# Attention and two MLPs on one core: loads that write 32 partitions each, issued half by SyncE and half by GpSimd

## The chip, the cores and the metric

The kernel runs on one core of one Trainium2 chip. The metric is device microseconds of one execution, from launch to end. Of the kernel before, three runs took 1405.77, 1406.9 and 1407.61 us; the median is 1406.9 us.

## What is computed

```python
def _attn_ref(u, v, z):                      # u, v: (2, 3008, 256), z: (2, 3008, 64)
    scores = (1.0 / S) * np.matmul(z, z.transpose(0, 2, 1))
    attn = np.maximum(scores, 0.0) ** 2
    return u * np.matmul(attn, v)

def _moe_ref(x, w_in, w_out, s, b):          # 6016 tokens, 256 -> 2048 -> 256
    r = np.maximum(x @ w_in, 0.0)
    return (s * (r * r) + b) @ w_out

def _moe2_ref(x, w_in, w_out):
    h = x @ w_in
    return (h * (1.0 / (1.0 + np.exp(-1.702 * h)))) @ w_out
```

The output is `_moe2_ref(_moe_ref(attention))`. Products on TensorE are made of two-part splits of float32 (a high part `hi` in float32r and the rest, `lo`), three matmuls for one product.

## The kernel before, in words

**Attention.** Each of the two batches has its 3008 tokens cut into six column chunks of 512 (the last has 448). For a query chunk `c` and a key chunk `kc`, four steps (`t`, 128 keys each) go through scores (L545, two matmuls into `ps_s`), relu and square on ScalarE (L549, L552), the split (`hi` L556 on ScalarE, `lo` L560 on VectorE) and six matmuls with `v` into an accumulator (L484, L485, L489). The scores are symmetric, so a block `(kc, c)` off the diagonal is computed once (`Fresh`), and its **mirror image** serves the other side: VectorE transposes the squared scores in 32x32 blocks into a tile `T` (L585), `park` stores it in HBM as `H` (L600, 128 partitions, 1 MB, from GpSimd's queue), and `fetch` (L604) loads it back as `R` in another arrangement: four DMAs of 256 KB, each to 32 of the 128 partitions (L613, from SyncE's queue). A `Turned` step then takes `hi` and `lo` out of `R` (L635, L639). `T` and `R` share five buffers of 1 MB (the pool `wide`); there are 15 such images in each batch.

**Other loads to 32 partitions.** `load_z` (L347) brings a chunk of `z` in four DMAs of 64 KB (runs of 128 bytes) to 32 partitions each, `load_v` (L420) a chunk of `v` in four DMAs of 128 KB (runs of 1 KB), `load_u` (L900) a chunk of `u` in four DMAs of 128 KB (runs of 256 bytes). All are SyncE's, but for the first chunks of `z` and `v`, shared with ScalarE's queue, and the other chunks of `v` in the first batch, which are GpSimd's and wait for `go`: a small copy on GpSimd (L400) after the first transposed `z`.

**Weights and MLPs.** The weights come as float64; VectorE and ScalarE decode them to float32 (`decode`, L656) and make sums and splits of them (`prepare`, L728) in the gaps of the attention and of the first MLP; GpSimd's queue stores these forms (L785 to L806), and SyncE's queue loads them for the MLPs (L815, L828, L842, L845). The two MLPs run from about 460 us to the end, in pairs of token chunks, with a seven-product scheme (L1088 up, L1256 and L1281 down).

**What sets the order.** Every piece of work is put on a list by `put` (L309) with its engine, its cost and the keys that it reads and writes; loads go through `moves` (L321), which gives them a transfer time `pipe`, scaled by a factor `slow`. A planner, `ordered` (L31), simulates the engines with these costs, free buffers and eight DMAs in flight in each of two sets (`lanes`, one for GpSimd's queue) and writes one order of all pieces. Each engine then runs its instructions in that order. In the built program the DMAs of a queue take eight semaphores in turn, so that a ninth waits for the landing of the first.

Of the kernel before, what the change touches and what calls it, by code (L numbers as in the profile page):

```python
# [20 lines left out]
class Op:  # L21


    def __init__(self, engine, cost, late, f, reads, writes, new, adds, free, due, pipe, soon, count):
        self.engine, self.cost, self.late, self.f = engine, cost, late, f
        self.reads, self.writes, self.new, self.adds = list(reads), list(writes), list(new), list(adds)
        self.free, self.due, self.pipe, self.soon, self.count = free, due, pipe, soon, count
        self.keys = list(dict.fromkeys(self.reads + self.writes + self.adds))


def ordered(ops, counts, clocks, reach, ahead, bulk, spread):  # L31
# [40 lines left out]
            before[users[new][0]].update(users[old])  # L72
    for i in range(n):
        before[i].discard(i)
        for j in before[i]:
            after[j].append(i)

    def lag(j, i):
        a = ops[j]
        if a.engine == ops[i].engine:  # L80
            return a.cost if a.engine == "PE" else a.cost + 0.1
        return a.cost + a.late
# [75 lines left out]
    while len(result) < n:  # L158
        best = None
        for e, now in clocks.items():  # L160
            among = [i for i in line[:reach] if not waiting[i]] if e == "PE" else pending[e]
            s0, pick = None, None
            soon = []
            for i in among:
                if best is not None and ready[i] >= best[0]:
                    continue
                t = start_of(i, now)
                if t is None:
                    continue
                t = max(t, now)  # L170
                rank = i if e == "PE" else latest[i]
                soon.append((rank, t, i))
                if s0 is None or t < s0 - 1e-9 or (t <= s0 + 1e-9 and rank < s0_rank):
                    s0, pick, s0_rank = t, i, rank
            if pick is not None and e in YIELD:
                limit = s0 + YIELD[e] * ops[pick].cost
                for rank, t, i in soon:
                    if t < limit and rank < s0_rank - WORTH and rank < t + URGENT:
                        s0, pick, s0_rank, limit = t, i, rank, 0.0 if t > s0 else limit
                        break  # L180
            if pick is not None and (best is None or s0 < best[0]):
                best = s0, pick, e
        if best is None:
            raise RuntimeError(f"no order: {len(result)} of {n}, {[(k, len(x)) for k, x in slots.items()]}, {left}")
        s0, i, e = best
        op = ops[i]
        end, late = s0 + op.cost, op.late
        if op.pipe:
            time, land, lane = s0, 0.0, lanes[e == "POOL"]
            for _ in range(op.count):  # L190
                time = max(time, lane.pop(0))
                pipe = max(pipe, time + 0.4) + op.pipe / op.count
                time += op.cost / op.count
                lane.append(max(time + 1.9, pipe + 1.7))
                land = max(land, lane[-1])
            end = time
            late = land - end
        clocks[e] = end
        (line if e == "PE" else pending[e]).remove(i)
        result.append(i)  # L200
        starts.append(s0)
        for key, kind in op.new:
            slots[kind].pop(0)
            needs[kind].remove((latest[i], i))
            if op.free and kind in left:
                left[kind] -= 1
                taken[key] = kind
        for key in op.keys:
            if key in uses:
                u = uses[key]  # L210
                u[1] -= 1
                u[2] = max(u[2], end + late)
                if u[1] == 0:
                    slots[u[0]].append(u[2])
                    if key in taken:
                        left[taken[key]] += 1
        for j in after[i]:
            waiting[j] -= 1
            t = end + late if op.pipe else s0 + lag(i, j)
            ready[j] = max(ready[j], t)  # L220
            if ops[j].free or op.engine != ops[j].engine:
                calm[j] = max(calm[j], t + (SLACK[0] if ops[j].free and op.pipe else SLACK[1] if op.pipe else SLACK[2]))
            if not waiting[j] and ops[j].engine != "PE":
                pending[ops[j].engine].append(j)
# [4 lines left out]
def attention_mlp_mlp_kernel(  # L229
# [74 lines left out]
        return bb * LASTC + c if c < LASTC else 2 * LASTC + bb  # L304


    ops, T = [], {}

    def put(engine, cost, late, f, reads=(), writes=(), new=(), adds=(), free=0, due=None, pipe=0, soon=None, count=1):  # L309
        ops.append(Op(engine, cost, late + pipe, f, reads, writes, new, adds, free, due, pipe, soon, count))  # L310

    def scalar(n, f, reads=(), writes=(), new=(), **more):
        put("ACT", 0.147 + 0.00072 * n, 0.15, f, reads, writes, new, **more)
# [7 lines left out]
    def moves(kb, fs, reads=(), writes=(), new=(), engine="SP", run=2048, count=None, slow=1.0, **more):  # L321
        def f():
            for g in fs:
                g()

        count = count or len(fs)
        pipe = 1.05 * slow * kb * 1024 / run * (0.0085 + run / 27200) / 16
        put(engine, (0.7 if engine == "POOL" else 0.45) * count, 2.0, f, reads, writes, new, pipe=pipe, count=count, **more)

    def move(kb, f, *args, **more):  # L330
        moves(kb, [f], *args, **more)
# [15 lines left out]
    def load_z(bb, t):  # L347
        n, z0, key = width(t), begin(bb, t), ("zr", bb, t)

        def tile_of():  # L350
            if key not in T:
                T[key] = cell(f"zr_{bb}_{t}").rearrange("p (t a) -> p t a", a=32)
            return T[key]

        fs = {"SP": [], "ACT": []}
        for i in range(4):
            q = slice(32 * i, 32 * i + 32)
            col = slice(32 * (i % 2), 32 * (i % 2) + 32)
            pieces = [(slice(0, n // 32), z0, n)]
            if n < CH:  # L360
                pieces.append((slice(n // 32, CH // 32), z0 + n - TAIL, TAIL))
            for cols, r0, r in pieces:
                on_act = (bb, t) == (0, 0) and i % 2

                def f(q=q, col=col, cols=cols, r0=r0, r=r, eng=nc.scalar if on_act else nc.sync):
                    eng.dma_start(
                        out=tile_of()[q, cols, :], in_=z[bb, r0 : r0 + r, col].rearrange("(t b) a -> b t a", b=32)
                    )

                fs["ACT" if on_act else "SP"].append(f)  # L370
        due = 0.0 if (bb, t) == (0, 0) else None
        moves(64 * len(fs["SP"]), fs["SP"], (), [key], [(key, "cell")], run=128, due=due)
        if fs["ACT"]:
            moves(128, fs["ACT"], (), [(key, 1)], (), engine="ACT", run=128, due=due)
# [45 lines left out]
    def load_v(bb, c):  # L420
# [13 lines left out]
            for half in range(2):  # L434
                pieces.append((slice(64 * half, 64 * half + 64), slice(3, 4), k0 + 3 * P, TAIL, "(t p) d -> p t d", dict(p=TAIL)))
        first = (bb, c) == (0, 0)
        queue = "POOL" if bb == 0 and c else "SP"
        fs = {"SP": [], "ACT": [], "POOL": []}
        for x, (rows_, ts, r0, r, how, dims) in enumerate(pieces):
            issuer = "ACT" if first and x % 2 else queue  # L440

            def f(rows_=rows_, ts=ts, r0=r0, r=r, how=how, dims=dims, issuer=issuer):
                eng = dict(SP=nc.sync, ACT=nc.scalar, POOL=nc.gpsimd)[issuer]
                eng.dma_start(out=tile_of()[rows_, ts, :], in_=v[bb, r0 : r0 + r, :].rearrange(how, **dims))

            fs[issuer].append(f)
        due = 0.05 if first else None
        gate = [("go",)] if queue == "POOL" else []
        moves(128 * len(fs[queue]), fs[queue], gate, [key], [(key, "big")], engine=queue, run=1024, slow=1.2, due=due)
        if fs["ACT"]:  # L450
            moves(256, fs["ACT"], (), [(key, 1)], (), engine="ACT", run=1024, slow=1.2, due=due)

    def permuted(x, order):
        return x.rearrange(f"p {order} -> p h i a", h=2, i=4)
# [149 lines left out]
    def fetch(bb, kc, c):  # L604
        H, key = ("H", bb, kc, c), ("R", bb, kc, c)
        fs = []
        for x in range(4):

            def f(x=x):
                if key not in T:  # L610
                    T[key] = wide_tile(f"R_{bb}_{kc}_{c}").rearrange("p (g q) -> p g q", g=4)
                src = T[H].rearrange("(g p) (b q) -> b p g q", g=4, b=4)[x]
                nc.sync.dma_start(out=T[key][32 * x : 32 * x + 32], in_=src)  # L613

            fs.append(f)
        moves(1024, fs, [H], [key], [(key, "wide")], slow=1.55)

    class Turned:
        def __init__(self, session, bb, t, kc, c):
# [280 lines left out]
    def load_u(m, due):  # L900
# [3 lines left out]
        for i in range(4):  # L904

            def f(i=i):
                if key not in T:
                    T[key] = big_tile(f"ur_{m}").rearrange("p (t a) -> p t a", a=64)
                nc.sync.dma_start(
                    out=T[key][32 * i : 32 * i + 32, : n // 32, :],  # L910
                    in_=u.rearrange("b s d -> (b s) d")[start : start + n, 64 * i : 64 * i + 64].rearrange(
                        "(t b) a -> b t a", b=32
# [1 line left out]
                )  # L914

            fs.append(f)
        moves(512, fs, (), [key], [(key, "big")], run=256, slow=1.25, due=due)

    def turn_u(m, h):
        n = tokens(m)[1]  # L920
# [738 lines left out]
```

## Time and profile before

| | us |
|---|---|
| median of three runs | 1406.9 |
| the profiled execution's own time | 1408.94 |
| its span, first to last instruction | 1407.2 |
| PE busy (matmuls) | 1387.8 |
| DVE busy | 1310.3 |
| ACT busy | 1190.0 |
| POOL busy | 148.6 |

The span is what the trace shows; what lies around it (1.74 us) is in the time alone. Rows "by stretch" give each engine's busy time between two moments of the span, the TensorE clock granted (1.00 is its full level), the busy share of the 16 DMA engines (over 1 where transfers overlap) and what they moved. PE counts as busy from a matmul's start to its modelled end.

### The profile page before, as it was taken

How to read it: one execution, taken by the hardware profiler on the slowest of the kernel's cores; microseconds unless marked ns; L12 is line 12 of the kernel's file. 1: busy time of each engine (PE TensorE's matmuls, PEld its weight loads, DVE VectorE, ACT ScalarE, POOL GpSimd, SP SyncE). 2: the span in 40 equal slices, each digit the busy share in tenths (PEclk: the TensorE clock that was granted, in tenths of full speed). 3: DMA queues.
4: the chain of work that ended last, by engine and by line, in shares of the span. 5: the costliest groups of instructions: out<-in, count | busy, mean ns of one | idle time of the engine just before them, and what ended most of it. 6: DMA issues, size and time to landing. Idle time of an engine off the chain costs nothing.

```text
span 1407.2 us, 20260 instructions
## 1 busy us (share of the span) xinstructions
PE 1387.8 (99%) x6147; PEld 1148.5 (82%) x6147; DVE 1310.3 (93%) x2324; ACT 1190.0 (85%) x2308; POOL 148.6 (11%) x235
## 2 busy tenths in 40 slices
PE   8999999999999999999999999999999999999998
PEld 5888779888888888787888888888888788888897
DVE  7999886999998699999999999999989999999987
ACT  8999675999877598998989899998878796978685
POOL 3022210002211000001010101100010101010010
PEclk9999999999999999999999999999999999999999
DMA  7899898869999556677768576866757575666553
GB/s 171 245 296 282 250 276 197 239 211 269 274 246 342 187 198 210 254 239 266 258 214 270 200 260 215 291 222 212 252 175 268 160 267 161 230 199 198 181 183 105
DMA packets 194829, 322.61 MB, mean 229 GB/s; under 512 B 85408, under 2 KB 117728, under 8 KB 190880
## 3 DMA queue, kind: packets, MB, share of 16 engines
q1 hardware_dynamic: 172976, 241.69, 57.4%
q0 software_dynamic: 19008, 78.90, 15.6%
q10 hardware_dynamic: 2736, 0.74, 0.3%
q8 instruction: 48, 0.79, 0.2%
q14 instruction: 61, 0.50, 0.1%
HBM read 244.19 MB, written 77.07 MB: 228 GB/s over the span
## 4 chain that ended last, share of the span: by engine, by line
PE 81%; issue 6%; DVE 4%; DMA 3%; ACT 3%; SPq 2%; ACTq 0%; POOL 0%; DVEq 0%; POOLq 0%
PE ps_b L1088 8%; PE ps_d L1088 8%; PE ps_c L1088 8%; PE accB L1281 6%; PE ps_s L545 5%; PE accA L485 4%; PE accA L484 4%; PE ps_d L1281 4%; PE accA L489 4%; PE ps_a L1088 4%; PE accB L484 4%; PE accB L485 4%; PE accB L489 4%; PE ps_b L1281 4%; PE accA L1281 3%
## 5 line engine op out<-in xcount | busy, mean ns | idle before, releaser
L1211 DVE TENSOR_TENSOR lo<-g_c,hi 128x512 fp32r<-128x512 f32 (+1 forms) x540 | 345.3, 672 | 6.4 <-ACT hi L1207 5.4
L1207 ACT CAST hi<-g_c 128x512 fp32r<-128x512 f32 (+1 forms) x540 | 310.9, 616 | 9.7 <-DVE g_c L1196 6.8
L1088 PE MATMUL ps_d<-op_t,up 128*128 128x512 f32 (+1 forms) x432 | 121.6, 390 | 2.0 <-DVE g_c L1162 1.7
L1088 PE MATMUL ps_b<-op_t,up 128*128 128x512 f32 (+1 forms) x432 | 121.3, 389 | 1.0 <-ACT s_u L1137 0.9
L549 ACT ACTIVATE a<-ps_s 128x512 f32<-128x512 f32 (+1 forms) x168 | 103.2, 621 | 21.4 <-PE ps_s L545 21.4
L484 PE MATMUL accA<-hi,v 128*128 128x512 f32 x288 | 112.7, 391 | 2.0 <-ACT hi L556 2.0
L1174 ACT ACTIVATE g_c<-g_c 128x512 f32<-128x512 f32 (+1 forms) x144 | 89.5, 622 | 29.2 <-DVE g_c L1162 28.7
L485 PE MATMUL accA<-hi,v 128*128 128x512 f32 x288 | 113.0, 392 | 0.0
L560 DVE TENSOR_TENSOR lo<-a,hi 128x512 fp32r<-128x512 f32 (+1 forms) x156 | 103.8, 668 | 9.7 <-ACT hi L556 8.6
L552 ACT ACTIVATE a<-a 128x512 f32<-128x512 f32 (+1 forms) x168 | 110.6, 665 | 0.9
L484 PE MATMUL accB<-hi,v 128*128 128x512 f32 (+1 forms) x288 | 110.0, 382 | 0.8 <-DVE hi L566 0.8
L485 PE MATMUL accB<-hi,v 128*128 128x512 f32 (+1 forms) x288 | 109.8, 381 | 0.0
L556 ACT CAST hi<-a 128x512 fp32r<-128x512 f32 (+1 forms) x168 | 108.2, 649 | 0.7
L1196 DVE TENSOR_TENSOR g_c<-g_c,g_c 128x512 f32<-128x512 f32 (+1 forms) x156 | 105.0, 673 | 1.4
L545 PE MATMUL ps_s<-zq,zk 128*128 128x512 f32 (+1 forms) x336 | 101.6, 390 | 2.8 <-DVE zk L394 2.2
L1088 PEld LDWEIGHTS ps_d<-op_t,up 128*128 128x128 f32 x432 | 79.5, 188 | 21.7 <-DVE g_c L1162 5.3
L1088 PEld LDWEIGHTS ps_b<-op_t,up 128*128 128x128 f32 x432 | 79.7, 188 | 19.9 <-DVE g_c L1162 2.8
L1281 PE MATMUL accB<-hi,d 128*128 128x512 f32 (+1 forms) x312 | 95.0, 386 | 0.0
L585 DVE STREAM_TRANSPOSE T<-a 128x512 f32<-128x512 f32 x120 | 83.9, 700 | 7.9 <-DMA H<-T 4.7
L1177 ACT ACTIVATE g_c<-g_c 128x512 f32<-128x512 f32 (+1 forms) x144 | 88.2, 629 | 0.6
L639 DVE TENSOR_TENSOR lo<-R,hi 128x512 fp32r<-128x512 f32 x120 | 79.4, 678 | 7.9 <-ACT hi L635 3.6
L489 PE MATMUL accA<-lo,v 128*128 128x512 f32 x276 | 85.8, 392 | 0.3 <-DVE lo L560 0.3
(181 smaller groups left out, 3418.9 us busy)
## 6 DMA issues: line engine op xcount, KB each, us to landing
up<-uf SPq DMA_DIRECT2D x96, 896.0 KB
H<-T POOLq DMA_DIRECT2D x30, 1024.0 KB, 7.5
R<-H SPq DMA_DIRECT2D x120, 256.0 KB
d<-dw SPq DMA_DIRECT2D x114, 256.0 KB
d_s<-df1s SPq DMA_DIRECT2D x54, 256.0 KB
d_s<-df0s SPq DMA_DIRECT2D x72, 128.0 KB
f<-rows SPq DMA_DIRECT2D x18, 512.0 KB
d_s<-df0s SPq DMA_DIRECT2D x36, 256.0 KB
```

What stands on the lines that cost most here:

```text
L484: nc.tensor.matmul(T[k][:, :n], w[:, 0, cols], T[hi][:, :n], **start_flags(k, fresh))
L485: nc.tensor.matmul(T[k][:, :n], w[:, 1, cols], T[hi][:, :n], **start_flags(k, ()))
L489: nc.tensor.matmul(T[k][:, :n], w[:, 0, cols], T[lo][:, :n], **start_flags(k, ()))
L545: nc.tensor.matmul(T[self.p][:, :n], k, T[zq][:, h, :n], start=h == 0, stop=h == 1)
L552: nc.scalar.activation(out=T[self.a][:, :n], in_=T[self.a][:, :n], func=AF.Square)
L556: nc.scalar.copy(out=T[self.hi][:, :n], in_=T[self.a][:, :n])
L560: nc.vector.tensor_tensor(out=T[self.lo][:, :n], in0=T[self.a][:, :n], in1=T[self.hi][:, :n], op=ALU.subtract)
L1088: nc.tensor.matmul(to[:, :n], a[h], y[:, g, :n], start=first and j == 0, stop=False, skip_group_check=True)
L1196: nc.vector.tensor_tensor(out=self.get(to), in0=self.get(x), in1=self.get(y), op=ALU.subtract)
L1207: nc.scalar.copy(out=T[keys[0]][:, :n], in_=self.get(c))
L1211: nc.vector.tensor_tensor(out=T[keys[1]][:, :n], in0=self.get(c), in1=T[keys[0]][:, :n], op=ALU.subtract)
L1281: nc.tensor.matmul(to[:, :n], w[:, h, cols], g[:, :n], start=first and j == 0, stop=False, skip_group_check=True)
```

## The change

The four DMAs of each image `R`, of each chunk of `u`, and of each chunk of `z` and `v` but the first are divided: two are issued by SyncE, two by GpSimd. For `R`, `u` and `z`, SyncE has partitions 0 to 63 and GpSimd 64 to 127; for `v` they take turns (0 to 31 and 64 to 95 SyncE's, the others GpSimd's). The planner treats the second half as a piece of its own that may start with the first, and its factors `slow` for these loads are lowered. In the first batch the GpSimd halves of `z` and `v` wait for `go`. The stores stay where they were.

```diff
+    def shared(kb, fs, reads, key, kind, gate=(), **more):
+
+        half = len(fs) // 2
+        moves(kb / 2, fs[:half], reads, [key], [(key, kind)], **more)
+        moves(kb / 2, fs[half:], list(reads) + list(gate), [(key, "half")], engine="POOL", second=True, **more)
+        halved[key] = (key, "half")
...
+        if ops[i].second:
+            before[i].add(i - 1)
...
+                eng = nc.scalar if on_act else nc.gpsimd if i >= 2 and (bb, t) != (0, 0) else nc.sync
...
+            shared(256, fs["SP"], (), key, "cell", [("go",)] if bb == 0 else (), run=128)
...
-        queue = "POOL" if bb == 0 and c else "SP"
...
-            issuer = "ACT" if first and x % 2 else queue
+            issuer = ("ACT" if first else "POOL") if x % 2 else "SP"
...
+                shared(512, halves_, (), key, "big", [("go",)] if bb == 0 else (), run=1024, slow=1.1)
...
-                nc.sync.dma_start(out=T[key][32 * x : 32 * x + 32], in_=src)
+                (nc.gpsimd if x >= 2 else nc.sync).dma_start(out=T[key][32 * x : 32 * x + 32], in_=src)
...
-        moves(1024, fs, [H], [key], [(key, "wide")], slow=1.55)
+        shared(1024, fs, [H], key, "wide", slow=1.2)
...
-                nc.sync.dma_start(
+                (nc.gpsimd if i >= 2 else nc.sync).dma_start(
...
-        moves(512, fs, (), [key], [(key, "big")], run=256, slow=1.25, due=due)
+        shared(512, fs, (), key, "big", run=256, slow=1.1, due=due)
```

In the whole program SyncE issues 740 DMAs instead of 851, and GpSimd 339 instead of 228. TensorE has 6147 matmuls in both, and ScalarE and VectorE have as many instructions as before.

**SyncE's queue, first batch, images of query chunk 4.** `R_0_4_2` is batch 0's image of block (4, 2), `wr_0_9` a weight block, `ur_3` a chunk of `u`, `vr_1_1` a chunk of batch 1's `v`. Before:

```order
L613 DMA R_0_4_1_1925<-H_0_4_1_1098 32x4x512 x4
L670 DMA wr_0_9_2045<-in_moe_w_in_dram 128x1x256 x2
L674 DMA wr_0_9_2045<-in_moe_w_out_dram 128x512
L909 DMA ur_3_2058<-in_u_dram 32x16x64 x4
L613 DMA R_0_4_2_2092<-H_0_4_2_1538 32x4x512 x4
L613 DMA R_0_4_3_2151<-H_0_4_3_1832 32x4x512 x4
L613 DMA R_0_5_0_2200<-H_0_5_0_786 32x4x512 x4
```

Now:

```order
L634 DMA R_0_4_1_1893<-H_0_4_1_1092 32x4x512 x2
L691 DMA wr_0_8_1928<-in_moe_w_in_dram 128x1x256 x2
L695 DMA wr_0_8_1928<-in_moe_w_out_dram 128x512
L691 DMA wr_0_9_1989<-in_moe_w_in_dram 128x1x256 x2
L695 DMA wr_0_9_1989<-in_moe_w_out_dram 128x512
L634 DMA R_0_4_2_2046<-H_0_4_2_1548 32x4x512 x2
L634 DMA R_0_4_3_2059<-H_0_4_3_1832 32x4x512 x2
L930 DMA ur_3_2122<-in_u_dram 32x16x64 x2
```

The images (4, 2) and (4, 3) now stand ahead of `ur_3`, and of each image two DMAs are left here.

**GpSimd's queue, the same place.** `H` are the images' stores, the others stores of weight forms and of gated rows. Before:

```order
L600 DMA H_0_4_3_1832<-T_0_4_3_1753 128x2048
L806 DMA df0s1_108<-forms_0_2_3_1820 128x2x128
L806 DMA df0s2_109<-forms_0_2_3_1820 128x2x128
L806 DMA df0s3_110<-forms_0_2_3_1820 128x2x128
L806 DMA df0s4_111<-forms_0_2_3_1820 128x2x128
L600 DMA H_0_5_3_1982<-T_0_5_3_1909 128x2048
L794 DMA dw03_94<-forms_0_3_2_1994 128x2x256 x2
L789 DMA uf03_78<-forms_0_3_1_1990 128x2x384
L785 DMA uf03_78<-forms_0_3_0_2063 128x1024
```

Now:

```order
L621 DMA H_0_4_3_1832<-T_0_4_3_1750 128x2048
L634 DMA R_0_4_0_1834<-H_0_4_0_709 32x4x512 x2
L827 DMA df0s1_108<-forms_0_2_3_1820 128x2x128
L827 DMA df0s2_109<-forms_0_2_3_1820 128x2x128
L827 DMA df0s3_110<-forms_0_2_3_1820 128x2x128
L827 DMA df0s4_111<-forms_0_2_3_1820 128x2x128
L634 DMA R_0_4_1_1893<-H_0_4_1_1092 32x4x512 x2
L621 DMA H_0_5_3_1982<-T_0_5_3_1902 128x2048
L634 DMA R_0_4_2_2046<-H_0_4_2_1548 32x4x512 x2
L810 DMA uf03_78<-forms_0_3_1_1987 128x2x384
L634 DMA R_0_4_3_2059<-H_0_4_3_1832 32x4x512 x2
L806 DMA uf03_78<-forms_0_3_0_2075 128x1024
```

The second halves of four images now stand between these stores, two of them ahead of the store `H_0_5_3`.

**GpSimd's queue at the start.** `zr_0_1` is the second chunk of `z`, `vr_0_1` the second of `v`. Before:

```order
L400 COPY going_121<-zt_0_0_184 128x1
L444 DMA vr_0_1_198<-in_v_dram 32x4x256 x4
L444 DMA vr_0_2_247<-in_v_dram 32x4x256 x4
L444 DMA vr_0_3_320<-in_v_dram 32x4x256 x4
L444 DMA vr_0_4_357<-in_v_dram 32x4x256 x4
```

Now:

```order
L416 COPY going_121<-zt_0_0_185 128x1
L379 DMA zr_0_1_179<-in_z_dram 32x16x32 x2
L379 DMA zr_0_2_182<-in_z_dram 32x16x32 x2
L459 DMA vr_0_1_187<-in_v_dram 32x4x256 x2
L379 DMA zr_0_3_199<-in_z_dram 32x16x32 x2
L459 DMA vr_0_2_207<-in_v_dram 32x4x256 x2
```

Half of each chunk of `z` after the first now comes behind the copy `going`.

VectorE's order moves too: when the last product with `u` is done (L952, the end of the attention), it has passed 261 instructions of `decode` and `prepare`, against 225 before; the rest of them follows in the first MLP.

## Rows read from the trace of the kernel before

**Rows 1.** The page: busy time and share of the span by engine.
```profile
PE 1387.8 (99%) x6147; PEld 1148.5 (82%) x6147; DVE 1310.3 (93%) x2324; ACT 1190.0 (85%) x2308; POOL 148.6 (11%) x235
```
**Rows 2.** By stretch (us): length; PE, PEld, DVE, ACT, POOL busy; clock, DMA, GB/s.
```profile
0.00:20.00 20.00, 16.66 (x59) 10.28 (x60) 12.14 (x23) 15.18 (x32) 11.42 (x26) 1.00 1.02 196
20.00:100.00 80.00, 79.03 (x345) 64.03 (x345) 78.95 (x154) 79.59 (x163) 11.14 (x18) 1.00 0.83 245
100.00:200.00 100.00, 96.62 (x414) 78.04 (x413) 91.79 (x182) 74.73 (x143) 21.16 (x32) 0.98 0.95 267
200.00:500.00 300.00, 300.00 (x1354) 253.51 (x1353) 264.15 (x487) 241.09 (x473) 40.74 (x62) 1.00 0.85 245
500.00:700.00 200.00, 196.51 (x859) 159.66 (x858) 193.97 (x343) 184.22 (x351) 14.02 (x21) 1.00 0.71 238
700.00:1200.00 500.00, 498.24 (x2209) 411.78 (x2208) 483.55 (x826) 434.82 (x837) 39.23 (x59) 1.00 0.68 228
1380.00:1407.20 27.20, 20.75 (x103) 18.89 (x101) 18.83 (x35) 11.64 (x25) 0.63 (x1) 0.93 0.38 101
```
**Rows 3.** PE in order of time: start, us, instruction, idle before and releaser.
```profile
153.57 0.73 PE L489 MATMUL accB<-lo,v 128*128 128x512 f32 x2 [0.41 <-DVE lo L560]
...
157.12 0.50 PE L484 MATMUL accB<-hi,v 128*128 128x512 f32 x1 [0.82 <-DVE hi L566]
...
187.23 0.50 PE L484 MATMUL accA<-hi,v 128*128 128x512 f32 x1 [2.03 <-ACT hi L556]
```
**Rows 4.** By stretch, around the idle time at 187 us.
```profile
184.00:187.20 3.20, 1.19 (x6) 0.65 (x4) 0.71 (x1) 3.17 (x7) 0.00 (x0) 1.00 1.08 230
187.20:191.90 4.70, 4.67 (x13) 3.60 (x14) 4.60 (x10) 4.70 (x11) 0.53 (x1) 0.64 1.14 217
```
**Rows 5.** ACT in order of time, at the same place.
```profile
184.03 0.62 ACT L635 CAST hi<-R 128x512 fp32r<-128x512 f32 x1 [4.19 <-DMA R<-H]
```
**Rows 6.** SP in order of time: `ur_3`, then three images.
```profile
160.58 11.99 SPq L909 DMA_DIRECT2D ur<-in_u_dram  x4
172.67 11.58 SPq L613 DMA_DIRECT2D R<-H  x12
```
**Rows 7.** By stretch, without engines: length, clock, DMA share, GB/s.
```profile
404.50:423.00 18.50, 1.00 1.11 224
424.00:433.00 9.00, 1.00 1.02 404
```
**Rows 8.** DVE in order of time, before the idle time at 153 us.
```profile
152.23 0.71 DVE L585 STREAM_TRANSPOSE T<-a 128x512 f32<-128x512 f32 x1 [4.70 <-DMA H<-T]
```
**Rows 9.** POOL by line: count, busy us, mean ns, idle before.
```profile
L1041 POOL DMA_DIRECT2D out_dram<-o x41 | 26.4, 651 | 422.2 <-DVE o L1024 362.6 <-DVE o L1029 58.5 <-issue 1.2
L444 POOL DMA_DIRECT2D vr<-in_v_dram x19 | 10.7, 568 | 1.8 <-DMA vr<-in_v_dram 1.7
```
**Rows 10.** POOL in order of time (start); tile `vr`, 5.5 to 7.2 us: landing.
```profile
5.53 0.44 POOL L400 COPY going<-zt 128x1 f32<-128x1 f32 x1 [4.65 <-DVE zt L382]
...
DMA to landing us min/median/max: 3.0/3.3/3.8
```
**Rows 11.** SP, DVE and PE in order of time, at the start.
```profile
3.07 17.41 SPq L366 DMA_DIRECT2D zr<-in_z_dram  x24
...
8.41 0.70 DVE L382 STREAM_TRANSPOSE zt<-zr 128x512 f32<-128x512 f32 x1
...
11.13 1.20 PE L545 MATMUL ps_s<-zq,zk 128*128 128x512 f32 x4 [1.53 <-DVE zk L394]
...
26.66 0.70 PE L545 MATMUL ps_s<-zq,zk 128*128 128x512 f32 x2 [0.68 <-DVE zk L394]
```
**Rows 12.** Waits: SP's for stores of images (total us, times, longest).
```profile
SPq L613 <- DMA H<-T: 91.4, 10, 16.8
```
**Rows 13.** Tile `H`, us from issue to landing; POOL in order of time.
```profile
DMA to landing us min/median/max: 4.2/7.5/10.9
...
125.00 0.55 POOL L600 DMA_DIRECT2D H<-T  x1 [7.27 <-DVE T L585]
```

More of the change, by code (lines that the diff above doesn't have):

```diff
@@ L21, with __init__ @@
 class Op:
-    def __init__(self, engine, cost, late, f, reads, writes, new, adds, free, due, pipe, soon, count):
+    def __init__(self, engine, cost, late, f, reads, writes, new, adds, free, due, pipe, soon, count, second):
         self.engine, self.cost, self.late, self.f = engine, cost, late, f
         self.reads, self.writes, self.new, self.adds = list(reads), list(writes), list(new), list(adds)
-        self.free, self.due, self.pipe, self.soon, self.count = free, due, pipe, soon, count
+        self.free, self.due, self.pipe, self.soon, self.count, self.second = free, due, pipe, soon, count, second
         self.keys = list(dict.fromkeys(self.reads + self.writes + self.adds))
@@ L79, in lag @@
         a = ops[j]
+        if ops[i].second and j == i - 1:
+            return 0.0
         if a.engine == ops[i].engine:
@@ L218, in ordered @@
             waiting[j] -= 1
-            t = end + late if op.pipe else s0 + lag(i, j)
+            t = s0 if ops[j].second and i == j - 1 else end + late if op.pipe else s0 + lag(i, j)
             ready[j] = max(ready[j], t)
-            if ops[j].free or op.engine != ops[j].engine:
+            if (ops[j].free or op.engine != ops[j].engine) and not (ops[j].second and i == j - 1):
                 calm[j] = max(calm[j], t + (SLACK[0] if ops[j].free and op.pipe else SLACK[1] if op.pipe else SLACK[2]))
@@ L304, in place, with put @@
         return bb * LASTC + c if c < LASTC else 2 * LASTC + bb
-    ops, T = [], {}
-    def put(engine, cost, late, f, reads=(), writes=(), new=(), adds=(), free=0, due=None, pipe=0, soon=None, count=1):
-        ops.append(Op(engine, cost, late + pipe, f, reads, writes, new, adds, free, due, pipe, soon, count))
+    ops, T, halved = [], {}, {}
+    def put(engine, cost, late, f, reads=(), writes=(), new=(), adds=(), free=0, due=None, pipe=0, soon=None, count=1, second=False):
+        reads = list(reads) + [halved[k] for k in reads if k in halved]
+        ops.append(Op(engine, cost, late + pipe, f, reads, writes, new, adds, free, due, pipe, soon, count, second))
     def scalar(n, f, reads=(), writes=(), new=(), **more):
@@ L363, in load_z, with f @@
                 on_act = (bb, t) == (0, 0) and i % 2
-                def f(q=q, col=col, cols=cols, r0=r0, r=r, eng=nc.scalar if on_act else nc.sync):
+                eng = nc.scalar if on_act else nc.gpsimd if i >= 2 and (bb, t) != (0, 0) else nc.sync
+                def f(q=q, col=col, cols=cols, r0=r0, r=r, eng=eng):
                     eng.dma_start(
@@ L371, in load_z @@
         due = 0.0 if (bb, t) == (0, 0) else None
+        if (bb, t) != (0, 0):
+            shared(256, fs["SP"], (), key, "cell", [("go",)] if bb == 0 else (), run=128)
+            return
         moves(64 * len(fs["SP"]), fs["SP"], (), [key], [(key, "cell")], run=128, due=due)
@@ L446, in load_v @@
             fs[issuer].append(f)
[L447 to L451, printed above, removed]
+        if not first:
+            halves_ = fs["SP"] + fs["POOL"]
+            if c < LASTC:
+                shared(512, halves_, (), key, "big", [("go",)] if bb == 0 else (), run=1024, slow=1.1)
+            else:
+                moves(384, fs["SP"], (), [key], [(key, "big")], run=1024, slow=1.1)
+                moves(64, fs["POOL"], [("go",)] if bb == 0 else (), [(key, "half")], engine="POOL", run=1024, second=True)
+                halved[key] = (key, "half")
+            return
+        moves(256, fs["SP"], (), [key], [(key, "big")], run=1024, slow=1.1, due=0.05)
+        moves(256, fs["ACT"], (), [(key, 1)], (), engine="ACT", run=1024, slow=1.1, due=0.05)
     def permuted(x, order):
```

## The prediction, made before the run

> **What bounds the kernel now.** I first read busy time by engine: TensorE is busy for 1387.8 of 1407.2 us [rows 1], so 19.4 us of idle time, and what the clock loses, are all that can be won. Then the same by stretch [rows 2], to see where they lie. TensorE is idle for 3.34 us in 0 to 20, 0.97 in 20 to 100, 3.38 in 100 to 200, nothing in 200 to 500, 3.49 in 500 to 700, 1.76 in 700 to 1200 and 6.45 in the last 27 us. The reader is to see that the loads in question are used only in the first 460 us, where 7.7 us are idle.
>
> Third, TensorE's own waits in 100 to 200 [rows 3]: 2.03 us at 187 us, 0.41 and 0.82 us at 153 to 157, together 3.26 of the 3.38. The clock row behind the long one is worth as much: after TensorE was busy for only 1.19 of 3.2 us, the granted clock is 0.64 on the mean for 4.70 us (levels 2.4 and 1.2 GHz) [rows 4], which loses 0.36 x 4.70 = 1.7 us. So this one wait costs 2.03 + 1.7 = 3.7 us.
>
> Fourth, what it waited for. ScalarE stood still for 4.19 us until an image had landed [rows 5]. SyncE spent 160.58 to 172.57 issuing the four DMAs of `ur_3`, with the images (4, 2), (4, 3) and (5, 0) behind them, then 11.58 us on their twelve [rows 6]. Four issues don't take 12 us by themselves; with eight DMAs on their way, each next one waits for a landing. The two waits at 153 come from VectorE, which stood 4.70 us for a buffer of `T` that an image's store still held [rows 8].
>
> Fifth, how fast images load. In 404.5 to 423 us, where SyncE issued nothing but images, 224 GB/s went with the DMA engines busy throughout (1.11); in 424 to 433, when a store from all 128 partitions ran beside them, 404 GB/s at 1.02 [rows 7]. So DMAs to 32 partitions, one after another, move at about half the rate that these engines have with traffic to other partitions.
>
> **The change, part by part.**
>
> *111 DMAs go from SyncE to GpSimd.* GpSimd has no issue price for loads of 64- or 32-element runs; the nearest rows are 0.57 us (`v`, 32x4x256) and 0.65 us (`out`, 32x16x64) [rows 9], so 111 x 0.57 to 0.65 = 63 to 72 us of GpSimd. It is busy 84.5 us in the first 500 [rows 2], and 72 more leave it idle for two thirds: nothing, as long as it doesn't wait with stores behind it (below). SyncE does nothing but issue, so its relief is worth only what lands earlier.
>
> *Images in two halves.* An image of 1 MB takes about 1.05 MB / 224 GB/s = 4.7 us now. With partitions 0 to 63 on one queue and 64 to 127 on the other it takes between 2.6 us (404 GB/s) and the same 4.7. I take the fast end, since the 404 GB/s row is these loads beside traffic to other partitions, as it will be. Then two images need 5 us instead of 9, and ScalarE's 4.19 us of waiting go; besides, the order puts (4, 2) and (4, 3) ahead of `ur_3`, which alone is up to 12 us. The 3.7 us go: **-3.7 us** (bounds -3.7 and 0).
>
> The Trainium skill speaks against this: "DMA: Bandwidth & Descriptors", section "Rules for kernel authors", says of two transfers to disjoint partition halves that one shouldn't bother, since they serialize on the same 16 DMA engines. The same skill's "SBUF — State Buffer", section "Door 1: The DMA port swizzle", says that partitions 0 to 63 hang on one half of the ports and 64 to 127 on the other. The pair of rows at 224 and 404 GB/s fits the second; no row shows two such loads side by side. By the first, the term above would shrink to what the order alone gives, which is the first rival.
>
> *The waits at 153 us.* They cost 1.23 us and came from a slow store. Faster images free buffers and DMA time; but the store's own queue now carries half images too. Half of it: **-0.6 us** (bounds -1.2 and +1.2).
>
> *The start.* Before, the second chunk of `z` was issued from 3.07 us on, and VectorE could transpose it at 8.41 without waiting; TensorE began with it at 11.13, having idled 1.53 us [rows 11]. Now half of it comes after the copy at 5.53 to 5.97 [rows 10]: its second DMA is issued at about 6.6 and lands 3.0 to 3.8 us later, if as the first loads of `v` did [rows 10]: near 10.4. The new order has TensorE start the values of the first chunk ahead of it, so about 0 to 1.5 us are lost there. Against this, 24 DMAs of `z` in 17.41 us become 12 on this queue, so later chunks come earlier: 0.68 us at 26.66 [rows 11], and 0.97 in all after 20 us [rows 2], may go. Net **0** (bounds -1.5 and +3).
>
> *Weights.* 36 more instructions of `decode` and `prepare` are done before the first MLP, in a stretch with VectorE at 264 of 300 us, and so fewer in 500 to 700, where it is busy 194 of 200 and TensorE idles 3.49 us [rows 2]. The rest of the order is shuffled too, so **-0.5** (bounds -2 and +2).
>
> *`u` and `v`:* `v` alternates, so its halves run mostly within the same 64 partitions at any time; nothing waits long for either, so nothing.
>
> The sum is -3.7 - 0.6 + 0 - 0.5 = -4.8 us. Against the profiled execution, 1408.94 us, it gives 1404.1; that execution lies 2.0 us over the median of the runs, 1406.9, so the forecast is **1402.1 us**. More than 14.6 us (7.7 + 5.25 + 1.7) can't be won, even if all idle time up to 1200 us and the slow clock went.
>
> **Rivals.**
>
> *No faster transfers.* If the halves only take turns, the images keep 4.7 us and the backlog of 100 to 200 (DMA share 0.95 [rows 2]) stays. Then the order's advance of the two images is eaten by the same full engines, and the wait of 3.7 us returns at this or the next image: 1406.9, or 1405 if half of it goes. For it: the DMA share over 1 in [rows 7] counts these engines as full. Against it: 404 GB/s with the same engines. 15%.
>
> *Slower: GpSimd waits for its own stores.* SyncE waited ten times, 91.4 us in all, for a store of an image to land before it could load one [rows 12]. The second halves now make GpSimd wait likewise, and there the next store stands behind: `H_0_5_3` behind two half images. A store lands in 7.5 us on the median and up to 10.9, and GpSimd got a new `T` 7.27 us after the last [rows 13]. A wait of the mean 9.1 us thus delays the next store by about 2 us, the longest, 16.8, by nearly 10; then VectorE waits for a buffer, as it did once for 4.70 us, which cost TensorE 1.23 us. It decides if more than three such waits come, since 3 x 1.23 = 3.7 us eat the gain. Six to ten among the 30 stores would be 7.4 to 12.3 us, less 3.7: 1410.6 to 1415.5. Against it: `T` and `R` share five buffers, and where SyncE waited now, the image wasn't due. 15%.
>
> *The order alone decides.* With every engine's order new, a few waits of 0.5 to 2 us in the MLPs come or go (5.25 us idle there): 1400 to 1409, and the likeliest value is my sum without the -0.5. 8%.
>
> **How the numbers follow.** My forecast has 62%, with a range of its own of 1399 to 1404.5. The range of 1398.5 to 1409 takes in the no-gain rival and the shuffles, and leaves out the slower rival's upper part and little below. A measurement can tell 0.2%, 2.8 us, from no change: up to 1404.1 is faster. The forecast gives 57 of its 62 to faster and 5 to same; the no-gain rival 2 and 13; the slower one 3 same, 12 slower; the shuffles 3, 3 and 2. That is 62% faster, 24% same, 14% slower.
>
> **What would show it.** The changed profile should show no wait of ScalarE for `R<-H` over 1 us, TensorE's idle time in 100 to 200 under 1 us and the clock at 1.00 there; images alone at well over 300 GB/s; SyncE's issue of three images in far less than 11.6 us. It would be wrong if the images still move at about 224 GB/s when alone, if VectorE's `T` waits for `H<-T` several times, or if the first 30 us hold more than 6 us of idle time.

## The result, and the profile after

The changed kernel takes 1422.8 us (median of 5 runs, 1420.1 to 1425.0) against 1406.9 us (1405.8 to 1407.9) of the kernel before: a ratio of 1.0114, interval 1.0099 to 1.0129. It is 15.9 us slower; the forecast was 1402.1 us, with a range of 1398.5 to 1409. The spans of the two profiled executions differ by 15.0 us (1422.2 against 1407.2), and those are followed up here.

Busy time by engine on the page of the changed kernel, against [rows 1]:

```profile
PE 1394.8 (98%) x6147; PEld 1152.8 (81%) x6147; DVE 1314.2 (92%) x2324; ACT 1189.7 (84%) x2308; POOL 215.4 (15%) x346
```

TensorE does the same 6147 matmuls, is busy 7.0 us longer and idle for 27.4 us instead of 19.4: 8.0 and 7.0 make the 15.0. By stretch, in the columns of [rows 2]:

```profile
0.00:20.00 20.00, 16.49 (x61) 10.33 (x62) 13.85 (x27) 15.32 (x32) 12.90 (x27) 1.00 0.99 206
20.00:100.00 80.00, 79.52 (x345) 63.88 (x344) 78.61 (x152) 79.78 (x164) 17.82 (x31) 1.00 0.78 244
100.00:200.00 100.00, 98.99 (x435) 81.30 (x435) 96.10 (x189) 79.58 (x153) 41.41 (x66) 1.00 0.98 286
200.00:500.00 300.00, 287.40 (x1253) 240.06 (x1252) 256.18 (x485) 223.71 (x441) 84.34 (x135) 0.96 0.82 238
500.00:700.00 200.00, 199.00 (x871) 161.95 (x870) 188.94 (x320) 183.07 (x350) 9.69 (x15) 1.00 0.64 222
```

Where a gain was forecast, there is one: 100 to 200 idles 1.01 us instead of 3.38 at a clock of 1.00, 500 to 700 idles 1.00 instead of 3.49. The loss lies where nothing was idle before: 12.6 us in 200 to 500. Four stretches of it, in the same columns:

```profile
205.00:208.00 3.00, 0.00 (x0) 0.00 (x0) 1.93 (x5) 0.00 (x0) 0.00 (x0) 0.79 1.02 226
208.00:217.00 9.00, 5.34 (x12) 3.75 (x13) 5.84 (x11) 3.95 (x8) 3.84 (x7) 0.50 0.94 210
...
236.00:238.00 2.00, 0.27 (x1) 0.27 (x2) 1.62 (x4) 1.16 (x3) 0.00 (x0) 0.86 0.64 116
238.00:247.00 9.00, 8.38 (x21) 6.13 (x22) 8.94 (x16) 6.90 (x17) 1.29 (x2) 0.50 0.35 66
```

Twice TensorE stands, and twice the clock is granted at 0.50 (its lower level, 1.2 GHz) for 9 us afterwards. 5.34 + 8.38 us of work at half speed cost 6.9 us, about the 7.0 us of longer busy time. What TensorE waited for in 200 to 250 (total us, times, longest), and behind it ScalarE (ACT) and VectorE (DVE) in order of time. Line numbers are those of the changed kernel, 21 above those of before (L505, L510, L577, L581, L656 and L706 are L484, L489, L556, L560, L635 and L685 there):

```profile
PE accA L510 <- DVE lo L581: 4.3, 1, 4.3
PE accA L505 <- ACT hi L577: 3.6, 1, 3.6
PE accB L510 <- DVE lo L581: 2.5, 1, 2.5
```
```profile
211.69 0.62 ACT L656 CAST hi<-R 128x512 fp32r<-128x512 f32 x1 [10.37 <-DMA R<-H]
```
```profile
206.07 0.43 DVE L706 TENSOR_SCALAR pw<-wr 128x512 uint32<-128x512 uint32 x1 [6.35 <-DMA vr<-in_v_dram]
...
236.38 0.43 DVE L706 TENSOR_SCALAR pw<-wr 128x512 uint32<-128x512 uint32 x1 [8.00 <-DMA wr<-in_moe_w_out_dram]
```

Two things come too late: an image, for which ScalarE stands 10.37 us, and two weight blocks. VectorE works in order, so a piece of `decode` (L706) that waits for `wr_10` or `wr_11` holds up the `lo` that TensorE needs. (The row at 206 us names a chunk of `v`, but L706 reads `wr` alone, and in 205 to 208 us SyncE's own next issue waits for that block:

```profile
SPq L634 <- DMA wr<-in_moe_w_out_dram: 1.1, 1, 1.1
```

so the weight block is what lands there.) SyncE's issues show why all three are late:

```profile
186.10 1.18 SPq L691 DMA_DIRECT2D wr<-in_moe_w_in_dram  x2
187.60 1.93 SPq L695 DMA_DIRECT2D wr<-in_moe_w_out_dram  x1
189.70 3.87 SPq L634 DMA_DIRECT2D R<-H  x2
193.68 6.79 SPq L459 DMA_DIRECT2D vr<-in_v_dram  x4
204.57 8.55 SPq L634 DMA_DIRECT2D R<-H  x6
213.60 9.04 SPq L459 DMA_DIRECT2D vr<-in_v_dram  x6
224.58 1.91 SPq L691 DMA_DIRECT2D wr<-in_moe_w_in_dram  x2
```

Weight block 10 stands ahead of image (5, 1), two chunks of `v` ahead of (5, 2) to (5, 4), and block 11 comes behind three more chunks of `v`. In the kernel before, SyncE issued (5, 1) to (5, 4) in one go, and block 10 only after `v` and `z` of the second batch:

```profile
195.26 18.50 SPq L613 DMA_DIRECT2D R<-H  x16
...
248.38 1.21 SPq L670 DMA_DIRECT2D wr<-in_moe_w_in_dram  x2
```

### The profile page after: what moved, and what is told of

Same layout as the page of the kernel before. It is cut to its first block, busy times and chain, and to the rows that moved or that the text cites. A ratio compares the mean times of both kernels' runs of the same rounds, so it can differ in the third digit from the quotient of the medians.

```text
span 1422.2 us, 20276 instructions
## 1 busy us (share of the span) xinstructions
PE 1394.8 (98%) x6147; PEld 1152.8 (81%) x6147; DVE 1314.2 (92%) x2324; ACT 1189.7 (84%) x2308; POOL 215.4 (15%) x346
## 4 chain that ended last, share of the span: by engine, by line
PE 68%; DMA 12%; DVE 9%; ACT 6%; issue 4%; POOL 1%; SPq 1%; DVEq 0%; ACTq 0%; POOLq 0%
PE ps_b L1109 7%; PE ps_d L1109 7%; PE ps_c L1109 7%; PE accB L1302 7%; PE ps_b L1302 4%; PE ps_d L1302 4%; PE ps_a L1109 4%; PE accA L1302 3%; PE ps_s L566 3%; DMA R<-H 3%; DMA wr<-in_moe_w_out_dram 3%; PE accB L505 3%; PE accB L506 3%; PE ps_c L1302 3%; PE accA L1277 2%
## 5 line engine op out<-in xcount | busy, mean ns | idle before, releaser
L505 PE MATMUL accA<-hi,v 128*128 128x512 f32 x288 | 113.6, 394 | 5.5 <-ACT hi L577 4.9
L505 PE MATMUL accB<-hi,v 128*128 128x512 f32 (+1 forms) x288 | 112.8, 392 | 2.4 <-DVE hi L587 2.3
L581 DVE TENSOR_TENSOR lo<-a,hi 128x512 fp32r<-128x512 f32 (+1 forms) x156 | 104.7, 672 | 9.2 <-ACT hi L577 8.5
L506 PE MATMUL accB<-hi,v 128*128 128x512 f32 (+1 forms) x288 | 112.3, 390 | 0.0
L577 ACT CAST hi<-a 128x512 fp32r<-128x512 f32 (+1 forms) x168 | 106.5, 635 | 0.5
L1062 POOL DMA_DIRECT2D out_dram<-o x41 | 26.4, 650 | 422.7 <-DVE o L1045 362.4
L510 PE MATMUL accA<-lo,v 128*128 128x512 f32 x276 | 86.1, 393 | 4.3 <-DVE lo L581 4.3
L656 ACT CAST hi<-R 128x512 fp32r<-128x512 f32 x120 | 69.9, 622 | 23.4 <-DMA R<-H 22.2
```

The lines of the kernel that those rows point to most:

```text
L505: nc.tensor.matmul(T[k][:, :n], w[:, 0, cols], T[hi][:, :n], **start_flags(k, fresh))
L506: nc.tensor.matmul(T[k][:, :n], w[:, 1, cols], T[hi][:, :n], **start_flags(k, ()))
L577: nc.scalar.copy(out=T[self.hi][:, :n], in_=T[self.a][:, :n])
L581: nc.vector.tensor_tensor(out=T[self.lo][:, :n], in0=T[self.a][:, :n], in1=T[self.hi][:, :n], op=ALU.subtract)
```

## Experiments: the order or the queue?

Two theories. *Order*: the lower factors `slow` make the planner believe that images move faster; it puts `v` and weights ahead of them, and they don't move faster. *Queue*: GpSimd's issue, its waits or its landings cost the time. The first run takes the factors alone:

```
- moves(1024, fs, [H], [key], [(key, "wide")], slow=1.55)    # u 1.25, v 1.2
+ moves(1024, fs, [H], [key], [(key, "wide")], slow=1.2)     # u 1.1, v 1.1
```

> The kernel before with one thing of the change alone: the planner's factors for how slowly loads of 32 partitions move (images 1.55 to 1.2, u 1.25 to 1.1, v 1.2 to 1.1). Every DMA stays where it was, on SyncE (v of the first batch on GpSimd). The order on SyncE becomes that of the changed kernel between the batches (ur_4 and v ahead of image (5, 0) and among (5, 1) and (5, 2), weight block 10 ahead of (5, 1)). Theory 'order' (the planner believes in faster loads, puts v and weights ahead of the last images, and TensorE stands): 1415 to 1427 us, over 8 us of TensorE idle in 200 to 250 and a granted clock under 0.9 there. Theory 'queue' (GpSimd's issue and landings cost the time): 1403 to 1409 us, no stall in 200 to 250.

1422.5 us, ratio 1.0103 (1.0086 to 1.0120): the whole loss, with not one DMA moved to another queue. (`wr_10` and the chunks of `v` stand on SyncE where the changed kernel has them.) TensorE in 200 to 250, in the columns of [rows 2], and ScalarE and VectorE in this run:

```profile
200.00:250.00 50.00, 38.82 (x162) 32.64 (x161) 27.32 (x49) 21.74 (x44) 1.08 (x2) 0.86 0.92 206
```
```profile
212.32 0.62 ACT L635 CAST hi<-R 128x512 fp32r<-128x512 f32 x1 [9.86 <-DMA R<-H]
```
```profile
208.04 0.43 DVE L685 TENSOR_SCALAR pw<-wr 128x512 uint32<-128x512 uint32 x1 [7.18 <-DMA vr<-in_v_dram]
```

11.18 us of idle time, where the changed kernel has 10.94, and the same two waits at the same place. Then the changed kernel's order with all halves on SyncE (`nc.gpsimd` becomes `nc.sync`, each first half issues all four):

> The changed kernel's order, with each second half issued by SyncE right behind the first half; GpSimd issues stores alone. Theory 'order': as the changed kernel or a little slower, 1416 to 1430 us, with the stall in 200 to 250. Theory 'queue': 1403 to 1410 us.

1426.8 us, ratio 1.0137 (1.0122 to 1.0152). And the reverse, the order of before with second halves on GpSimd:

```
+ (nc.gpsimd if x >= 2 else nc.sync).dma_start(...)   # images; u, z alike, v by x % 2
```

> The kernel before with its own order of every operation, but each second half of z, u, v and the images is issued by GpSimd (v alternately), at the same place in the order. Theory 'order': 1403 to 1411 us, about as before. Theory 'queue': 1413 us or more. Beside this it shows the rate of images alone in halves (404 to 423 us of the kernel before): about 224 GB/s if the halves only take turns, over 300 GB/s if, as the prediction had it, other partitions add rate.

1412.9 us, ratio 1.0038 (1.0023 to 1.0053): a little above the range of *order*, at the edge of that of *queue*. In the old order the queues cost 5.2 us; in the new they give some 3 to 4 back (1.0137 with them taken away, 1.0114 in the change; the intervals overlap). So the order is worth 10 to 19 us, the queues 5 at most, either way. The largest part of the 5.2 us is one wait, with which 100 to 200 idles 8.87 us instead of 3.38:

```profile
191.83 0.79 PE L484 MATMUL accA<-hi,v 128*128 128x512 f32 x1 [8.87 <-ACT hi L556]
```

ScalarE stood for an image 9.46 us here, 4.19 before [rows 5]. Two queues can have twice as many DMAs on their way, so the image due next would share the engines with later ones. That reading is only argued; it fits the run below in which images are fast and this wait is gone.

The change with the old factors:

> The changed kernel with the old factors (images 1.55, u 1.25, v 1.2); the halves stay split between SyncE and GpSimd. One load of v fewer stands ahead of the images (5, 2) to (5, 4), weight block 10 still ahead of (5, 1). Theory 'order': the stall in 200 to 250 shrinks but doesn't go, 1407 to 1416 us. Theory 'queue': as the changed kernel, 1419 to 1426 us.

1430.5 us, ratio 1.0162 (1.0147 to 1.0178): slower still, and neither theory's number. The planner, told of two queues, still puts weight block 10 ahead of (5, 1). TensorE idles 6.6 us in 100 to 200, 8.0 in 200 to 250, and 6.95 in 500 to 700, where the change idles 1.0. So the old factors alone don't mend the order: lower factors are enough for the loss, as the first run shows, but not needed for it. What misleads the planner here stays open.

## Experiments: how fast do images move?

The prediction leaned on [rows 7]. What moved in their second stretch, 424 to 433 us of the kernel before, by queue (q0 is GpSimd's, q1 SyncE's; packets, MB, share of 16 engines):

```profile
q0 software_dynamic: 647, 2.40, 66.2%
q1 hardware_dynamic: 665, 1.22, 35.8%
```

Of the 404 GB/s, two thirds are GpSimd's stores; the images moved at 136. What did improve is the engine time per byte: 0.358 x 16 x 9 us for 1.22 MB is 42 ns per KB. Images alone, 413 to 416 us, took 1.055 x 16 x 3 us for 0.67 MB, 76 ns per KB:

```profile
q1 hardware_dynamic: 365, 0.67, 105.5%
```

And in halves on two queues (the order of before, 413 to 422 us):

```profile
q1 hardware_dynamic: 650, 1.13, 60.7%
q0 software_dynamic: 266, 0.89, 44.6%
```

That is 77 ns per KB on SyncE's queue, 72 on GpSimd's, 224 GB/s in all: **the halves take turns**, and nothing is gained. What does hold the images? The next run keeps order, queue and the addresses read, and writes each DMA to all 128 partitions (the line taken out is given in short):

```
- T[key][32 * x : 32 * x + 32] <- b p g q piece x of T[H]
+ nc.sync.dma_start(out=T[key][:, x], in_=T[H][:, 512 * x : 512 * x + 512])
```

> The kernel before, same order and queue, but each of the four DMAs of an image writes 2 KB to each of all 128 partitions instead of 8 KB (four runs of 2 KB) to each of 32. It reads the same addresses in the same DMA; the blocks land without the exchange of partitions, so the second half of the mirrored products is not the reference's. Tells what holds images at about 224 GB/s when nothing else moves. If writing to 32 partitions at a time does: images alone run at over 300 GB/s in 410 to 421 us, SyncE issues faster, the wait of TensorE at 187 us shrinks, 1401 to 1406 us. If the reading of 2 KB pieces or the engines' own rate does: 200 to 250 GB/s as before, 1404 to 1410 us.

1400.5 us, ratio 0.9947 (0.9930 to 0.9964). Then 64 partitions per DMA, neighbours (`[64 * h : 64 * h + 64]`) or every other one (`[h::2]`):

> As the run with wide images (the same part of the computation changed), but each of the four DMAs writes to 64 partitions, 0 to 63 or 64 to 127, in two runs of 2 KB each. If the number of partitions in a DMA sets the rate in proportion, it lies between 225 and 390 GB/s; if partitions 0 to 63 reach no more ports than 0 to 31 do, at 200 to 240 GB/s, and the time is that of before, 1403 to 1409 us.

> As the run with 64 neighbouring partitions, but each DMA writes to the even or to the odd ones of all 128: again 64 partitions, two runs of 2 KB each. If ports decide: 350 to 400 GB/s and 1399 to 1403 us. If the number of partitions decides: as the run with 64 neighbouring ones.

Neighbours: 1405.9 us, ratio 0.9996 (0.9985 to 1.0006). Every other one: 1399.8 us (2 runs), ratio 0.9947 (0.9927 to 0.9967). Images alone in the kernel before (410 to 421 us), with 128 partitions, with 64 neighbours and with 64 even ones, in the columns of [rows 2]:

```profile
410.00:421.00 11.00, 11.00 (x50) 9.12 (x49) 10.94 (x25) 6.89 (x14) 1.00 (x2) 1.00 1.06 224
```
```profile
403.00:407.50 4.50, 4.50 (x21) 3.75 (x20) 4.50 (x12) 3.41 (x7) 0.00 (x0) 1.00 1.06 387
```
```profile
410.00:419.00 9.00, 9.00 (x42) 7.44 (x41) 8.94 (x20) 6.80 (x13) 0.55 (x1) 1.00 1.07 226
```
```profile
401.00:404.00 3.00, 3.00 (x15) 2.49 (x14) 3.00 (x7) 0.00 (x0) 0.00 (x0) 1.00 1.03 382
```

224, 387, 226, 382 GB/s. Not the number of partitions decides, but which: 64 neighbours are as slow as 32, 64 spread ones as fast as 128. The Trainium skill bears on this in "SBUF — State Buffer", section "Door 1: The DMA port swizzle": partitions 0 to 63 reach no more ports than 0 to 31. The four rows agree.

Then two queues, each on its own half, should add, and don't. Two more pairings: quarters dealt out so that both queues are meant to write to the same half at a time, and one queue that alternates between the halves:

> The run with the order of before and split halves (1412.9 us), but an image's quarters are dealt out in turn: SyncE issues partitions 0 to 31 and 64 to 95, GpSimd 32 to 63 and 96 to 127, so that what runs at the same time on the two queues lies in the same half of SBUF. If the two queues take turns packet by packet: the same rate, 210 to 240 GB/s for images alone, and 1408 to 1416 us. If the pairing of the split run gained something from reaching both halves: under 200 GB/s here, and slower than 1413 us.

> The kernel before with an image's four DMAs issued in the order of partitions 0, 64, 32, 96, all by SyncE. If the 16 engines go through a queue in step: 220 to 235 GB/s for images alone and 1404 to 1410 us. If they drift apart, so that some write to the one half while others write to the other: over 260 GB/s and under 1405 us.

```profile
416.00:425.00 9.00, 9.00 (x41) 7.45 (x41) 8.94 (x20) 6.80 (x13) 2.83 (x6) 1.00 1.06 245
```
```profile
404.00:413.00 9.00, 9.00 (x42) 7.44 (x41) 8.94 (x20) 6.79 (x13) 0.56 (x1) 1.00 1.06 241
```

1412.3 us at 245 GB/s (ratio 1.0036, 1.0020 to 1.0052) on the same half, if the two queues keep step, which the trace doesn't show; 224 on different ones: pairing different halves gains nothing. Alternating gave 241 GB/s, 8% over 224, and 1403.6 us (ratio 0.9971, 0.9954 to 0.9988), the rate between the two expectations, the time within the second. It changes only the order of four issues, leaves nothing of the reference out, and is already faster than the kernel before. The Trainium skill has the rule that the prediction weighed and set aside ("DMA: Bandwidth & Descriptors", "Rules for kernel authors"): transfers to disjoint halves serialize, also from two issuing engines; these runs agree. Why the same 16 engines can't serve both halves at once, though beside stores an image's packet takes half the time, stays open.

## Experiments: if the images were fast

The factors alone, with images over 128 partitions; and the split, with images to even and odd partitions:

> The kernel of the factors alone (all on SyncE, images believed faster; 1422.5 us) with the images loaded over 128 partitions as in the run with the order of before (that part of the computation differs in the same way). If loads over 128 partitions are as fast as the planner now believes, this order is right for them: the stall at 200 to 250 mostly goes, 1403 to 1412 us. If they aren't faster, or if what stalls TensorE there is VectorE behind pieces of weight block 10, not the images: 1416 to 1426 us.

> The order of before and the split of z, u, v and images between SyncE and GpSimd, but an image's DMAs write to the even partitions (SyncE) or the odd ones (GpSimd), as in the unsplit run with 64 even partitions (1399.8 us; that part of the computation differs in the same way). If two queues cost nothing by themselves: 1398 to 1403 us. If GpSimd's issue, its waits or its landings cost time: 1404 us or more, with a wait of ScalarE for an image or of VectorE for a buffer in 100 to 200.

1404.5 us (ratio 0.9974, 0.9963 to 0.9984) and 1401.0 us (0.9953, 0.9937 to 0.9968). With fast images the order that cost 15 us costs 4 (1404.5 against 1400.5), and the queues cost 1 (1401.0 against 1399.8), which is within the noise of the two ratios. So neither costs much by itself: each does while images need 4.7 us of all engines. The second case in 100 to 200, where the split of slow images lost 8.87 us:

```profile
100.00:200.00 100.00, 100.00 (x443) 82.81 (x442) 99.12 (x194) 82.69 (x159) 44.21 (x68) 1.00 0.90 294
```

Last, the planner's factor the other way, with the split (2.0) and without (1.8):

> The changed kernel's split with u and v at the old factors (1.25, 1.2) and the images planned as slower than before (2.0 instead of 1.55): SyncE's order then has the images (5, 1) to (5, 4) ahead of all v of the second batch and no weight block among them. Theory 'order': no stall over 2 us in 200 to 250, 1403 to 1414 us, and what is left over 1407 is in 100 to 200 as in the run with the order of before. Theory 'queue': 1415 us or more wherever the halves are split.

> The kernel before, nothing split, with the images planned as slower (1.8 instead of 1.55). A check that the planner's factor for images works in both directions: if the old factor was right, 1405 to 1412 us; if it was still too fast, the wait at 187 us goes and 1402 to 1405 us.

1411.9 us (ratio 1.0022, 1.0008 to 1.0036), with no idle time at all in 100 to 250: the loss of the change is gone, but 6.45 us of idle time appear in 250 to 460, not where *order* had put them. Without the split 1405.0 us (0.9981, 0.9970 to 0.9993), a time on the border of the two expectations. The trace leans to the second: in 100 to 200 TensorE no longer waits for ScalarE behind an image, but 2.1 us for VectorE.

## A version that beats both

The fast runs above leave the exchange of partitions out. The first try to keep it brings one row of blocks to 128 partitions in each DMA, the second does `v` alike:

```
+ src = T[H].rearrange("(g p) (b q) -> g b p q", g=4, b=4)[x]
+ nc.sync.dma_start(out=T[key][:, x], in_=src)
```

> The kernel before, order, queue and number of DMAs unchanged; the exchange of partitions is kept, but each of an image's four DMAs now brings one row of blocks to all 128 partitions (2 KB each) instead of all rows to 32 partitions. If the partitions of one DMA set the rate: as the run with wide images, 1399 to 1403 us, images alone at over 350 GB/s. If it was the order of the reads in memory that the wide run had made easier: 1404 to 1408 us and under 300 GB/s.

> The run with images by rows of blocks, and v in the same way: each of its four DMAs brings 1 KB to all 128 partitions instead of 4 KB to 32. Same order. If v was ever waited for, or its slow loads held up images: 0.5 to 3 us under the run with images by rows; if not, within 1 us of it.

1558.4 us (ratio 1.1076, 1.1060 to 1.1093) and 1587.5 us (1.1280, 1.1261 to 1.1298), both far outside what was expected. Images alone in the first, 270 to 275 us:

```profile
270.00:275.00 5.00, 5.00 (x26) 4.57 (x25) 1.93 (x4) 2.19 (x4) 0.00 (x0) 1.00 0.26 102
```

102 GB/s at a DMA share of 0.26, that of four of 16 engines. The Trainium skill has the rule ("DMA: Bandwidth & Descriptors", "Why a DMA increments its semaphore by 16 and not by 1"): the outermost dimension of both patterns sets how many engines a DMA uses, and here the source's is 4; the share agrees. So the exchange goes to the store, whose four pieces keep 32 outermost, and the loads read memory in one piece:

```
+ T[H] = hbm.tile([4 * P, CH], ...)
+ for g in range(4):
+     to_hbm.dma_start(out=T[H][P * g : P * g + P].rearrange("(b p) q -> p b q", b=4),
+                      in_=T[key][32 * g : 32 * g + 32].rearrange("p b s r -> p b (s r)"))
- nc.sync.dma_start(out=T[key][32 * x : 32 * x + 32], in_=src)
+ nc.sync.dma_start(out=T[key][:, x], in_=T[H][P * x : P * x + P])
```

> The kernel before, same order, with the exchange of partitions moved from the load of an image to its store: GpSimd stores four times 32 partitions (2 KB runs) instead of once 128 (8 KB runs), and SyncE's four loads each bring 2 KB to all 128 partitions from memory that lies in one piece. All of the reference is computed. If stores from 32 partitions are held at half the rate too, the time is shifted from the loads to the stores: 1403 to 1412 us. If stores don't suffer, as the runs with wide images: 1399 to 1403 us. GpSimd issues 90 DMAs more, about 51 us in 460.

1401.7 us, ratio 0.9955 (0.9942 to 0.9969): 6 us faster than before, 21 than the change, with the old order and nothing split. Images alone run at 377 GB/s, and 100 to 200 is full:

```profile
100.00:200.00 100.00, 100.00 (x442) 82.66 (x441) 97.90 (x193) 81.29 (x156) 34.78 (x55) 1.00 0.96 298
...
409.00:413.00 4.00, 4.00 (x20) 3.30 (x19) 3.94 (x8) 3.69 (x8) 1.08 (x2) 1.00 1.05 377
```

The stores do pay for it. Queues over the whole span (packets, MB, share of 16 engines), before and in this run:

```profile
q1 hardware_dynamic: 172976, 241.69, 57.4%
q0 software_dynamic: 19008, 78.90, 15.6%
...
q1 hardware_dynamic: 172976, 241.69, 54.1%
q0 software_dynamic: 24288, 78.91, 17.9%
```

For the same bytes GpSimd's queue takes some 500 us of engine time more (17.9% of 16 x 1400.2 us against 15.6% of 16 x 1407.2) and SyncE's some 800 less. The kernel is faster all the same: TensorE no longer waits for the loads, and VectorE doesn't wait for one of these stores, as it did before for 4.70 us [rows 8].

## Why the prediction was wrong, point by point

- *What bounds the kernel*: right. 3.26 us of waits and the slow clock in 100 to 200 could be won; the runs with fast images win them (100.00 of 100 busy), and come out 6 to 7 us faster.
- *Images in two halves*: **the step that failed**. "I take the fast end, since the 404 GB/s row is these loads beside traffic to other partitions, as it will be." Two thirds of that row were stores; a split by queue would have told. Halves move at 224 GB/s, as the rival without faster transfers and the Trainium skill's rule had it; "about 224 GB/s when alone" stood among the signs of being wrong.
- That the 3.7 us at 187 went all the same came from the order, which has those images ahead of `ur_3`. The step named both causes; only the second was there: the run of the factors alone and the one with the changed kernel's order, both with everything on SyncE, don't have this wait for an image either (their 1.8 and 3.3 us of waits in 100 to 200 are for VectorE). So the term's number came true by its lesser cause: luck.
- *What was left out*, **a term put at nothing**: the price of the new order. It was read at the places where it helped (the images ahead of `ur_3`), not at the seam of the batches, where weight block 10 and `v` came ahead of (5, 1) to (5, 4). The table by stretch [rows 2] showed no idle time there, so I priced nothing; but an order is right for the rates it was planned with. That is 10.9 of the 12.6 us (200 to 250 is busy for 39.06 of 50) and the two stretches at the lower clock. The two failures hang together: with images loaded fast, over 128 partitions, the order of the factors gave 1404.5 us, inside the range.
- *Weights*, -0.5 (-2 to +2): 500 to 700 gained 2.5 us, and VectorE is busy 5.0 us less there (188.94, 193.97 in [rows 2]). That the second is why isn't shown: with images over 128 partitions the old order gains 2.1 us there (198.64 busy) with VectorE busier (196.56). Pieces of this kind, done earlier, are what VectorE stood for at 206 and 236 us: the term had a gain and not its cost.
- *The start*, 0: the number right, 0.17 us more idle time to 20 us, 0.49 less to 100. *The waits at 153 us*, -0.6: the number right, 0.58 us instead of 1.23, but not for its reason, as images weren't faster; VectorE waits 3.06 us for a buffer of `T` instead of 4.70. *111 issues of GpSimd*: 215.4 - 148.6 = 66.8 us, within the 63 to 72, and hidden.
- *Rivals*: "No faster transfers" had the cause right and the time wrong, since it let the order cost nothing: the wait did return at a later image, much as it said, but with 10.37 us of ScalarE instead of 4.19. "GpSimd waits for its own stores" forecast slower by another mechanism; VectorE's `T` waited for a store only once (3.1 us). "The order alone decides" named the mechanism of the loss, but looked for it in the MLPs, with 1409 us at most.

## What to carry to other kernels

A rate read from a stretch with several streams belongs to none of them: take it per queue, in engine time per byte, before a load's price is set by it. A planner's cost is a promise: lowering it reorders work far from the edit, and if the chip doesn't keep it, the loss shows where nothing was idle. Where loads to a block of partitions are slow, spread each DMA over all of SBUF with a long outermost dimension on both sides, rather than spreading the DMAs over queues.

## What the runs showed of the hardware

- Writes to 64 neighbouring partitions run at 226 GB/s, to 64 even ones at 382, to 128 at 387; an exchange of blocks put into the store cost some 500 us of DMA engine time, and no time of the kernel that these runs show.
- A second queue that writes to the other half adds nothing (224 GB/s), yet beside stores an image's packets take 42 ns of engine time per KB instead of 76.
- Loads whose source has an outermost dimension of 4 run at a DMA share of 0.26 and 102 GB/s, and cost this kernel 152 us.
